# Float64 weights converted in pieces of twice the size, in place, with new lists of steps (Mamba2 SSD, then a SwiGLU feed-forward)

## The chip, the cores and the metric

The kernel runs on one core of one Trainium2 chip. The metric is the device time of one execution in microseconds. The kernel before was timed four times: 417.78, 417.67, 417.70 and 418.24 us, a median of 417.74.

## The reference, cut to what matters

Inputs: x (4, 8, 768, 32), a (4, 8, 768), B and C (4, 8, 768, 16) in float32; the three weight matrices arrive in float64, that is in words of eight bytes, and the gain rms_g in float32. The first part is a state-space recurrence, worked in chunks of 32 here (any size of chunk gives the same values):

```python
for c in range(nc):
    cum = np.cumsum(la, axis=-1)                          # la = log a in the chunk
    L = np.exp(cum[..., :, None] - cum[..., None, :]) * causal
    M = np.einsum('bhin,bhjn->bhij', Cc, Bc) * L
    y[:, :, sl] = (np.einsum('bhij,bhjd->bhid', M, xc)
                   + np.einsum('bhin,bhnd->bhid', Cc, state) * np.exp(cum)[..., None])
    Bx = np.einsum('bhjn,bhjd->bhjnd', Bc, xc) * np.exp(cum[..., -1:] - cum)[..., None, None]
    state = np.exp(np.sum(la, -1))[:, :, None, None] * state + np.sum(Bx, axis=2)
```

The second part takes y as 3072 tokens of 256 numbers:

```python
xn = x / np.sqrt(np.mean(x * x, -1, keepdims=True) + 1e-6) * rms_g
g = xn @ w_gate                                           # 256 x 1536
out = (g / (1 + np.exp(-g)) * (xn @ w_val)) @ w_out       # 1536 x 256
```

## The kernel before, in words

**Tiles and blocks.** The recurrence is worked in 12 pairs of 128-token chunks, the feed-forward in six blocks of 512 tokens, so two pairs make a block. While a block's feed-forward runs, the recurrence of the next block's two pairs is put between its matmuls; block 0 does the first four pairs itself. All code is one function with many small nested ones, and nothing is ordered by a scheduler: every block has a hand-written **list of steps** (block 0 at L950, block 1 at L1022, blocks 2 to 4 at L1049, block 5 at L1075). A step is a word such as `gate.2`; the loop at L978 (L1096 for the other blocks) calls its function, which issues the step's instructions to the queues of their engines. Each engine runs its own queue in the order of the list and waits where an operand, or the space for a result, isn't ready.

**The steps of the recurrence** (pair p, half or chunk i): `d`/`c` sums of logarithms (L329, L339), `dx`/`cx` their exponentials on ACT (L332, L343); `mask`, `sums`, `exp` the decay matrix of half a pair (L363; L374 and L379; ACT L386); `turn` transposes B and C through PE (L434), `T`, `Tt` copy the result out (L440, L442; DVE L912 in pair 0, ACT L909 after it); `g` and `gg` the products C times B (L468), `L` and `L1` their product with the decays (DVE L478, L489); `A` and `S` the states (PE L501; DVE L513, L519 to L523); `y` the outputs (L541, L550); `sq`, `yt` take y out. `scale` multiplies B and C by decays (DVE L419). For later pairs the decays come from memory instead: `row` and `rowout` write sums to DRAM, `spread` (a DMA on SP's queue, L393) reads them back, `sub` and `ex` make the decays of them.

**Norm and feed-forward of block 0.** `ms`, `mc`, `mt`, `rs`, `rb`, `rc`, `xn` make the normalised tokens (PE L591, ACT L597, PE L600, DVE L605 and POOL L607, PE L613, ACT L618, DVE L629). `early` (PE L658) multiplies the first two column blocks of the weights with tokens not yet normalised, and `norm` (DVE L669) puts the factor on afterwards. `gate.f` (PE L648, eight passes of 128x512) makes gate and value of 128 columns, `silu.f` (ACT L674 or L676) and `hid.f` (DVE L681) the hidden rows. For the second half of the columns (j = 3 to 5), as in all later blocks, the product is made of seven half-size products with sums before and after: `cw` (DVE L702) makes sums of weights, `tx` (DVE L709) differences of tokens; `P.k.j` (PE L732) one product, `take` (ACT L738) and `C` (DVE L744) its totals, `silug` (ACT L753) and `hidg` (DVE L757) the hidden rows. `o` (PE L764) is the last projection of block 0; the later blocks project with `O` (PE L815), from sums of weights `two` (DVE L778) and of hidden rows `s` to `s4` (DVE L788 to L798).

**Weights.** A piece of the float64 matrices is fetched as 32-bit words (`fetch`, L134, SP's queue) and converted in three steps: `pow.k` makes the power of two out of the top 16 bits (three ACT instructions, L167, L168, L170); `man.k` makes the mantissa (DVE L177 puts the top 20 bits in place, DVE L180 adds the low word); `wt.k` multiplies the two into the weight tile (DVE L186) and issues the next fetch. There are 20 pieces: four of 128x256 numbers and sixteen of 128x512, each of one matrix only. Nine are fetched at the start. The mantissa has a tile of its own (`m`, two slots); the fetched words have slots of their own (`ws`, four; `wr`, six), the powers four (`e`).

**Slots that make waits.** PSUM is split into three slots of two banks, used in turn by `mask`, `g`, `y`, `early`, `gate` (`take` at L870 picks the slot that was left first, `leave` gives it back), and two single banks ("one", L82) used in turn by `turn`, `A`, `ms`, `rb`, `row`, the sums of logarithms and two of the four results of `gg`. Two of the three slots are handed over to the `P` products by `switch`. A step that takes a slot waits until the reader of the earlier tenant is done: `gate` for an `exp` or a `silu`, a `turn` for the DVE step that read the bank. `load.p` issues six DMAs with the inputs of pair p (L107, L113).

**Start.** `make_identity`, masks and constants are made on DVE and POOL (L210 to L260), each in a tile of its own; 12 matmuls of zeros (L266) run before the first inputs have landed.

Of the kernel before, what the change touches and what calls it, by code (L numbers as in the profile page):

```python
# [9 lines left out]
FP32 = mybir.dt.float32  # L10
I32 = mybir.dt.int32
I16 = mybir.dt.int16
U32 = mybir.dt.uint32
BF16 = mybir.dt.bfloat16
# [6 lines left out]
def kernel(  # L21
# [98 lines left out]
    def words(w):  # L120
# [7 lines left out]
    wdst = {"g": wg, "v": wv, "o": wo}  # L128
    pieces = [(n, c, w) for c, w in [(0, 128), (128, 128)] + [(c, 256) for c in range(256, DF, 256)]
              for n in "gv"]  # L130
    pieces += [("o", c, 2) for c in range(0, NF, 2)]
    fetched = []

    def fetch(k=1):  # L134
        for _ in range(min(k, len(pieces))):
            n, c, w = pieces.pop(0)
            if n == "o":
                src, dst, shape = wsrc[n][:, c:c + w], wo[:, c:c + w], (w, DM)
            else:
                src, dst = wsrc[n][:, :, 2 * c:2 * (c + w)], wdst[n][:, :, c:c + w]  # L140
                shape = (2, w)
            small = shape[0] * shape[1] == 256
            r = raw.tile([P, shape[0], 2 * shape[1]], I32, tag="ws" if small else "wr",
                         name="wr", bufs=4 if small else 6)
            nc.sync.dma_start(out=r, in_=src)
            w32 = r.rearrange("p k (f w) -> p k f w", w=2)
            w16 = r.bitcast(I16).rearrange("p k (f w) -> p k f w", w=4)
            fetched.append((w16[:, :, :, 3], (w32[:, :, :, 0], w32[:, :, :, 1]), dst,
                            [P] + list(shape)))
# [10 lines left out]
    def power(k):  # L160
        words16, (lo, hi), dst, shape = fetched[k]
        n = shape[1] * shape[2]
        e = cvt.tile([P, n], FP32, tag="e", name="e", bufs=4)
        k16 = e.bitcast(I16)[:, n:2 * n].rearrange("p (a b) -> p a b", a=shape[1])
        g = e.rearrange("p (a b) -> p a b", a=shape[1])
        b16 = e.bitcast(I16)[:, 0:n].rearrange("p (a b) -> p a b", a=shape[1])
        nc.scalar.activation(out=k16, in_=words16, func=AF.Relu, scale=1.0 / 16, bias=kinks[:, 0:1])  # L167
        nc.scalar.activation(out=g, in_=k16, func=AF.Prelu, scale=-1.0, bias=kinks[:, 1:2],  # L168
                             alpha=2.0 ** -20)
        nc.scalar.activation(out=b16, in_=g, func=AF.Prelu, scale=-2.0 ** 27, bias=kinks[:, 2:3],  # L170
                             alpha=2.0 ** -20)
        parts[k, "e"] = b16.bitcast(BF16)

    def mantissa(k):
        words16, (lo, hi), dst, shape = fetched[k]
        m = cvt.tile(shape, I32, tag="m", name="m")
        nc.vector.tensor_scalar(out=m, in0=hi, scalar1=0xFFFFF, scalar2=0x100000,  # L177
                                op0=ALU.bitwise_and, op1=ALU.bitwise_or)
        parts[k, "f"] = f = m.bitcast(FP32)
        nc.vector.scalar_tensor_tensor(out=f, in0=lo.bitcast(U32), scalar=2.0 ** -32, in1=m,  # L180
                                       op0=ALU.mult, op1=ALU.add)

    def weight(k):
        words16, (lo, hi), dst, shape = fetched[k]
        e, f = parts.pop((k, "e")), parts.pop((k, "f"))
        nc.vector.scalar_tensor_tensor(out=dst, in0=f, scalar=2.0 ** -20, in1=e,  # L186
                                       op0=ALU.mult, op1=ALU.mult)
        fetch()

    warm = const.tile([P, 256], BF16, name="warm")  # L190
# [8 lines left out]
    fetch(2)  # L199
    gcol = const.tile([P, 2], FP32, name="gcol")  # L200
    nc.sync.dma_start(out=gcol, in_=moe_rms_g.rearrange("(t p) -> p t", p=P))
    fetch(4)
    load(2)
    load_x(2)
    fetch(3)
# [6 lines left out]
    ones = const.tile([P, P], FP32, name="ones")  # L212
    nc.vector.memset(ones, 1.0)
    zeros = const.tile([P, P], FP32, name="zeros")
    nc.vector.memset(zeros, 0.0)
    upto = const.tile([P, P], FP32, name="upto")
    nc.gpsimd.affine_select(out=upto, in_=ones, pattern=[[1, P]], compare_op=ALU.is_ge,
                            fill=0.0, base=0, channel_multiplier=-1)
    never = const.tile([P, P], FP32, name="never")
    nc.gpsimd.affine_select(out=never, in_=zeros, pattern=[[1, P]], compare_op=ALU.is_ge,  # L220
                            fill=-2.0 ** 100, base=0, channel_multiplier=-1)
    after = const.tile([P, P], FP32, name="after")
# [72 lines left out]
    mids = const.tile([P, 2, P], FP32, name="mids")  # L295
# [395 lines left out]

    def combine_w(j):
# [436 lines left out]
```

## Time and profile before

The profile was taken in an execution of its own. Its time was 418.28 us; the profiled span, from the first to the last instruction, is 416.6 us of it.

| view | what it shows |
| --- | --- |
| timed runs | 417.67 to 418.24 us, median 417.74 |
| profiled execution | 418.28 us, span 416.6 us, granted clock of PE 0.999 |
| waits that end PE's idle time | one in the chain of the end: PE idle L266 |
| DMA traffic | 27.99 MB, 24.22 read and 3.28 written in HBM |
| conversion on ACT (L167, L168, L170) | 14.3, 13.6 and 13.6 us in 20 instructions each |
| conversion on DVE (L177, L180) | 7.9 and 12.8 us in 20 instructions each |

PE is TensorE, PEld its weight loads, DVE VectorE, ACT ScalarE, POOL GpSimd, SP the engine whose queue issues most DMAs. In the table of windows each row is a stretch of the span, with the busy time of each engine and its instructions in brackets, then PE's granted clock, the busy share of the DMA engines and GB/s. In a group row the columns are line, engine, operation, result and operands, shapes and count, then busy us and mean ns of one, then the engine's idle time before them and what ended it. A timeline row has start, duration, engine, line and operation. The ends of matmuls are modelled, so the distance from one start to the next says more of PE than the busy time does.

### The profile page before, as it was taken

What the parts mean: (1) busy time and instruction counts of PE and PEld (TensorE: products, weight loads), DVE (VectorE), ACT (ScalarE), POOL (GpSimd) and SP (SyncE); (2) the same over time, 40 slices, a digit from 0 to 9 for tenths busy, and PEclk for the clock granted to TensorE, in tenths of its full rate; (3) what the DMA queues carried; (4) which work ended last, traced back from release to release, by engine and by line L of the source; (5) the groups of instructions that cost most, each with busy time, mean ns of one, the idle gap of its engine ahead of it and who ended that gap; (6) DMA issues with size and microseconds to landing.
All of it is one profiled execution on the core that took longest, in us unless ns stands there. A gap on an engine that the chain in (4) does not pass through costs nothing.

```text
span 416.6 us, 7930 instructions
## 1 busy us (share of the span) xinstructions
PE 411.9 (99%) x3100; PEld 345.0 (83%) x3100; DVE 304.1 (73%) x665; ACT 229.7 (55%) x462; POOL 39.0 (9%) x48
## 2 busy tenths in 40 slices
PE   8999999999999999999999999999999999999996
PEld 5665468888878899888899887899888889988896
DVE  5899998979679986376986477795476684547671
ACT  2998998877646316745428645526646521245410
POOL 3020000023000005000013100014100000000000
PEclk9999999999999999999999999999999999999999
DMA  9899849001007122703070502070100000100001
GB/s 110 225 207 174 238 117 364 8 0 51 2 2 151 30 74 40 112 2 101 9 146 25 77 2 101 2 148 6 53 2 0 2 2 1 52 0 2 0 2 50
DMA packets 86564, 27.99 MB, mean 67 GB/s; under 512 B 76000, under 2 KB 80352, under 8 KB 86528
## 3 DMA queue, kind: packets, MB, share of 16 engines
q1 hardware_dynamic: 82368, 27.24, 27.9%
q10 hardware_dynamic: 4160, 0.26, 0.8%
q8 instruction: 24, 0.39, 0.4%
q14 instruction: 12, 0.10, 0.1%
HBM read 24.22 MB, written 3.28 MB: 66 GB/s over the span
## 4 chain that ended last, share of the span: by engine, by line
PE 99%; DVE 0%; issue 0%
PE gate L732 28%; PE o L815 23%; PE val L732 21%; PE o L764 5%; PE g L468 4%; PE gate L648 3%; PE y L550 3%; PE tp L434 2%; PE y L541 2%; PE gate L658 2%; PE e L363 1%; PE A_ps L501 1%; PE e L374 1%; PE rb L613 1%; PE idle L266 1%; PE ms L591 1%
## 5 line engine op out<-in xcount | busy, mean ns | idle before, releaser
L744 DVE TENSOR_TENSOR c<-val,p 128x512 f32<-128x512 f32 x99 | 67.3, 686 | 49.8 <-PE val L732 37.5
L738 ACT COPY p<-gate 128x512 f32<-128x512 f32 x99 | 57.8, 588 | 68.1 <-PE gate L732 62.9
L732 PE MATMUL gate<-tx,sw 128*128 128x256 f32 x264 | 65.0, 382 | 0.0
L732 PEld LDWEIGHTS gate<-tx,sw 128*128 128x128 f32 x264 | 48.7, 190 | 8.2 <-issue 2.0
L757 DVE TENSOR_TENSOR h<-c 128x256 f32<-128x256 f32 x99 | 41.0, 431 | 19.1 <-ACT c L753 19.0
L753 ACT ACTIVATE c<-c 128x256 f32<-128x256 f32 x99 | 38.2, 413 | 11.5 <-DVE c L744 10.7
L732 PE MATMUL val<-xn,sw 128*128 128x256 f32 x132 | 34.1, 383 | 0.0
L732 PE MATMUL val<-tx,sw 128*128 128x256 f32 x132 | 33.9, 384 | 0.0
L815 PE MATMUL o<-wo,h 128*128 128x128 f32 x240 | 33.7, 277 | 0.0
L732 PE MATMUL gate<-tx,wgv 128*128 128x256 f32 x132 | 33.1, 381 | 0.0
L732 PE MATMUL val<-xn,wgv 128*128 128x256 f32 x132 | 33.1, 379 | 0.0
L732 PE MATMUL gate<-xn,wgv 128*128 128x256 f32 x132 | 33.0, 380 | 0.0
L815 PE MATMUL o<-two,s 128*128 128x128 f32 x240 | 32.0, 275 | 0.0
L569 POOL TENSOR_TENSOR sq<-sq 128x256 f32<-128x256 f32 x12 | 10.1, 840 | 226.9 <-ACT sq L568 196.9
L815 PE MATMUL o<-two,h 128*128 128x128 f32 x240 | 30.9, 275 | 0.0
L815 PEld LDWEIGHTS o<-wo,h 128*128 128x128 f32 x240 | 29.9, 192 | 1.0 <-issue 0.6
L815 PEld LDWEIGHTS o<-two,s 128*128 128x128 f32 x240 | 29.9, 192 | 0.3
L827 ACT COPY v<-o 128x256 f32<-128x256 f32 x15 | 5.6, 373 | 43.6 <-PE o L815 43.6
L815 PEld LDWEIGHTS o<-two,h 128*128 128x128 f32 x240 | 28.9, 192 | 0.1
L732 PEld LDWEIGHTS val<-tx,sw 128*128 128x128 f32 x132 | 24.5, 190 | 4.6 <-DVE h L757 1.0
L732 PEld LDWEIGHTS val<-xn,sw 128*128 128x128 f32 x132 | 24.4, 190 | 4.2 <-issue 0.7
L732 PEld LDWEIGHTS gate<-tx,wgv 128*128 128x128 f32 x132 | 24.8, 190 | 3.5 <-issue 0.2
(158 smaller groups left out, 700.7 us busy)
## 6 DMA issues: line engine op xcount, KB each, us to landing
L<-rowd SPq DMA_DIRECT2D x16, 512.0 KB, 4.7
xr<-in_x_dram SPq DMA_DIRECT2D x24, 128.0 KB, 3.5
wr<-in_moe_w_out_dram SPq DMA_DIRECT2D x6, 512.0 KB, 6.7
wr<-in_moe_w_gate_dram SPq DMA_DIRECT2D x5, 512.0 KB, 6.1
wr<-in_moe_w_val_dram SPq DMA_DIRECT2D x5, 512.0 KB, 5.9
out_dram<-ob SPq DMA_DIRECT2D x10, 256.0 KB, 2.1
br<-in_B_dram SPq DMA_DIRECT2D x22, 64.0 KB, 4.2
cr<-in_C_dram SPq DMA_DIRECT2D x22, 64.0 KB, 3.3
```

What stands on the lines that cost most here:

```text
L434: nc.tensor.transpose(out=tp[:, k], in_=src[:, i].rearrange("p h n -> p (h n)"), identity=ident)
L468: nc.tensor.matmul(out=g[:, 256 * i:256 * i + 256], lhsT=T[r, i, 0], rhs=T[r, i, 1:3].rearrange("p t m -> p (t m)"), start=(i == 0), stop= ...
L550: nc.tensor.matmul(out=y[o:o + 32, h // 4, i * P:(i + 1) * P], lhsT=s["x"][:, i, h], rhs=Ls[p][:, i, h], start=opens, stop=True, tile_posi ...
L569: nc.gpsimd.tensor_tensor(out=sqs[blk][:, tk], in0=sq2[:, 0], in1=sq2[:, 1], op=ALU.add)
L648: nc.tensor.matmul(out=gv[:, k], lhsT=w[:, t, fs], rhs=xns[0][:, t], start=(t == 0), stop=(t == 1))
L732: nc.tensor.matmul(out=dst[:, half[w]], lhsT=lhsT, rhs=rhs, start=(k in (1, 2, 5) and w == 0), stop=True, skip_group_check=True)
L738: nc.scalar.copy(out=t, in_=Xs[j])
L744: nc.vector.tensor_tensor(out=t, in0=Zs[j], in1=a, op=ALU.add)
L753: nc.scalar.activation(out=u, in_=src[:, half[0]], func=AF.Silu)
L757: nc.vector.tensor_tensor(out=hidden_tile(blk, j)[:, c // 10 - 1, c % 10 - 1], in0=u, in1=src[:, half[1]], op=ALU.mult)
L764: nc.tensor.matmul(out=o, lhsT=hs_[blk, f // 2][:, f % 2, k // 2, (k % 2) * P:(k % 2 + 1) * P], rhs=wo[:, f], start=opens, stop=(f == NF - ...
L815: nc.tensor.matmul(out=o[:, t * P:(t + 1) * P], lhsT=lhsT[:, t], rhs=rhs, start=(k in (1, 2, 4, 5) and j == 0 and t == 0), stop=True, skip ...
```

## The change

**Pieces.** Ten pieces in the place of twenty: two of 128x512 numbers and eight of 128x1024. Gate and value of the same columns make one piece, filled by two DMAs; the output matrix comes in pieces of four rows of blocks, not two. Five pieces are fetched at the start, and a new one only after `wt.2` and later ones. Small pieces lie in the slots of the hidden rows ("h"), large ones in three slots ("wr"), the powers in two; the tiles that `take` fills have four slots of their own ("p"). The numbers behind `pow`, `man` and `wt` now count these pieces.

**Mantissas.** They get no tile: both DVE instructions write into the fetched words, every second word of the tile, the first over the high and the second over the low words.

**Constants and sums.** Seven early constants (the zeros of the first matmuls, `ones`, `zeros`, `upto`, `never`, `after`, `mids`) become parts of one tile in the slot of the output tile "ob". The six tiles with sums of weights (`cw.0` to `cw.2` and three `two`) lie in pairs in three slots of "wr".

**Lists.** All four lists of steps are new. Apart from `pow`, `man` and `wt` with numbers from 10 on, block 0 has the same steps as before, and the others have them too. In the diff below the list of block 0 is shown up to the steps of pair 3's outputs; the other lists, the rest of the constants and the new form of two operand choices (L809 to L813) are left out.

```diff
-    wdst = {"g": wg, "v": wv, "o": wo}
-    pieces = [(n, c, w) for c, w in [(0, 128), (128, 128)] + [(c, 256) for c in range(256, DF, 256)]
-              for n in "gv"]
-    pieces += [("o", c, 2) for c in range(0, NF, 2)]
+    pieces = [("gv", c, 128) for c in (0, 128)] + [("gv", c, 256) for c in range(256, DF, 256)]
+    pieces += [("o", c, 4) for c in range(0, NF, 4)]
     fetched = []
 
     def fetch(k=1):
         for _ in range(min(k, len(pieces))):
             n, c, w = pieces.pop(0)
+            if w == 128:
+                r = ffn.tile([P, 8 * w], I32, tag="h", name="wr", bufs=NF // 2)
+            else:
+                r = raw.tile([P, 8 * 256], I32, tag="wr", name="wr", bufs=3)
             if n == "o":
-                src, dst, shape = wsrc[n][:, c:c + w], wo[:, c:c + w], (w, DM)
+                nc.sync.dma_start(out=r.rearrange("p (o m) -> p o m", o=w),
+                                  in_=wsrc[n][:, c:c + w])
+                dst = wo[:, c:c + w].rearrange("p o m -> p (o m)")
             else:
-                src, dst = wsrc[n][:, :, 2 * c:2 * (c + w)], wdst[n][:, :, c:c + w]
-                shape = (2, w)
-            small = shape[0] * shape[1] == 256
-            r = raw.tile([P, shape[0], 2 * shape[1]], I32, tag="ws" if small else "wr",
-                         name="wr", bufs=4 if small else 6)
-            nc.sync.dma_start(out=r, in_=src)
-            w32 = r.rearrange("p k (f w) -> p k f w", w=2)
-            w16 = r.bitcast(I16).rearrange("p k (f w) -> p k f w", w=4)
-            fetched.append((w16[:, :, :, 3], (w32[:, :, :, 0], w32[:, :, :, 1]), dst,
-                            [P] + list(shape)))
+                both = r.rearrange("p (n t f) -> p n t f", n=2, t=2)
+                for k, name in enumerate("gv"):
+                    nc.sync.dma_start(out=both[:, k], in_=wsrc[name][:, :, 2 * c:2 * (c + w)])
+                dst = wgv[:, :, :, c:c + w]
+            w32 = r.rearrange("p (f w) -> p f w", w=2)
+            fetched.append((r.bitcast(I16).rearrange("p (f w) -> p f w", w=4)[:, :, 3],
+                            w32[:, :, 0], w32[:, :, 1], dst, w32.shape[1]))
...
-        words16, (lo, hi), dst, shape = fetched[k]
-        n = shape[1] * shape[2]
-        e = cvt.tile([P, n], FP32, tag="e", name="e", bufs=4)
-        k16 = e.bitcast(I16)[:, n:2 * n].rearrange("p (a b) -> p a b", a=shape[1])
-        g = e.rearrange("p (a b) -> p a b", a=shape[1])
-        b16 = e.bitcast(I16)[:, 0:n].rearrange("p (a b) -> p a b", a=shape[1])
+        words16, lo, hi, dst, n = fetched[k]
+        e = cvt.tile([P, n], FP32, tag="e", name="e", bufs=2)
+        k16, b16 = e.bitcast(I16)[:, n:2 * n], e.bitcast(I16)[:, 0:n]
         nc.scalar.activation(out=k16, in_=words16, func=AF.Relu, scale=1.0 / 16, bias=kinks[:, 0:1])
-        nc.scalar.activation(out=g, in_=k16, func=AF.Prelu, scale=-1.0, bias=kinks[:, 1:2],
+        nc.scalar.activation(out=e, in_=k16, func=AF.Prelu, scale=-1.0, bias=kinks[:, 1:2],
                              alpha=2.0 ** -20)
-        nc.scalar.activation(out=b16, in_=g, func=AF.Prelu, scale=-2.0 ** 27, bias=kinks[:, 2:3],
+        nc.scalar.activation(out=b16, in_=e, func=AF.Prelu, scale=-2.0 ** 27, bias=kinks[:, 2:3],
                              alpha=2.0 ** -20)
-        parts[k, "e"] = b16.bitcast(BF16)
+        parts[k] = b16.bitcast(BF16)
+
 
     def mantissa(k):
-        words16, (lo, hi), dst, shape = fetched[k]
-        m = cvt.tile(shape, I32, tag="m", name="m")
-        nc.vector.tensor_scalar(out=m, in0=hi, scalar1=0xFFFFF, scalar2=0x100000,
+        words16, lo, hi, dst, n = fetched[k]
+        nc.vector.tensor_scalar(out=hi, in0=hi, scalar1=0xFFFFF, scalar2=0x100000,
                                 op0=ALU.bitwise_and, op1=ALU.bitwise_or)
-        parts[k, "f"] = f = m.bitcast(FP32)
-        nc.vector.scalar_tensor_tensor(out=f, in0=lo.bitcast(U32), scalar=2.0 ** -32, in1=m,
-                                       op0=ALU.mult, op1=ALU.add)
+        nc.vector.scalar_tensor_tensor(out=lo.bitcast(FP32), in0=lo.bitcast(U32),
+                                       scalar=2.0 ** -32, in1=hi, op0=ALU.mult, op1=ALU.add)
 
     def weight(k):
-        words16, (lo, hi), dst, shape = fetched[k]
-        e, f = parts.pop((k, "e")), parts.pop((k, "f"))
+        words16, lo, hi, dst, n = fetched[k]
+        f, e = lo.bitcast(FP32), parts.pop(k)
+        if len(dst.shape) > 2:
+            f, e = [v.rearrange("p (n t f) -> p n t f", n=2, t=2) for v in (f, e)]
         nc.vector.scalar_tensor_tensor(out=dst, in0=f, scalar=2.0 ** -20, in1=e,
                                        op0=ALU.mult, op1=ALU.mult)
-        fetch()
-
-    warm = const.tile([P, 256], BF16, name="warm")
+        if k > 1:
+            fetch()
+
+
+    start = ffn.tile([P, 8, P], FP32, tag="ob", name="start", bufs=1)
+    warm = start[:, 0].bitcast(BF16)
...
         load_x(p)
-    fetch(2)
+    fetch(1)
     gcol = const.tile([P, 2], FP32, name="gcol")
     nc.sync.dma_start(out=gcol, in_=moe_rms_g.rearrange("(t p) -> p t", p=P))
-    fetch(4)
+    fetch(2)
     load(2)
     load_x(2)
-    fetch(3)
+    fetch(2)
     load(3)
     load_x(3)
 
 
     ident = const.tile([P, P], FP32, name="ident")
...
+    spaces = []
+
+    def piece_for_sums(k):
+        while len(spaces) <= k // 2:
+            spaces.append(raw.tile([P, 2, 8 * P], FP32, tag="wr", name="sums", bufs=3))
+        return spaces[k // 2][:, k % 2]
+
     def combine_w(j):
         if j < NF // 4:
-            s = raw.tile([P, 2, 4, P], FP32, tag="wr", name="sw", bufs=6)
+            s = piece_for_sums(j).rearrange("p (w k m) -> p w k m", w=2, k=4)
...
-        vs[k, j] = t = cvt.tile([P, 512], FP32, tag="e", name="p", bufs=4)
+        vs[k, j] = t = cvt.tile([P, 512], FP32, tag="p", name="p", bufs=4)
...
-        two[j0 // 2] = w = raw.tile([P, 4, 2, P], FP32, tag="wr", name="two", bufs=6)
+        two[j0 // 2] = w = piece_for_sums(3 + j0 // 2).rearrange("p (k j m) -> p k j m", k=4, j=2)
...
     order = """
-        load.4 mask.0.0 r.0 parts.0 c mask.0.1 turn.0.1 cx T.0.1 Tt.0.1.0 turn.0.0 sums.0.1 cc d
-        turn.1.1 exp.0.1 Tt.0.1.1 sums.0.0 T.0.0 Tt.0.0.0 Tt.0.0.1 dx T.1.1 mask.1.1 scale.1
-        Tt.1.1.0 Tt.1.1.1 exp.0.0 turn.1.0 g.0.1 last.1 T.1.0 sums.1.1 Tt.1.0.0 scale.0 g.0.0
-        last.0 L.0.1 Tl.1 Tt.1.0.1 A.0 exp.1.1 L.0.0 Tl.0 man.0 mask.1.0 pow.0 g.1.1 S.0 row.1
-        pow.1 L.1.1 sums.1.0 A.1 wt.0 exp.1.0 g.1.0 S.1 pow.2 y.0 sq.0 pow.3 r.1 L.1.0 man.1 y.1
-        yt.0 wt.1 sq.1 ydone.0 early.0.0 man.2 rowout.1 pow.4 parts.1 scale.2 ms.0 yt.1 mask.2.0
-        mc.0 turn.2.0 T.2.0 man.3 Tt.2.0.0 pow.5 sums.2.0 ydone.1 mt.0 exp.2.0 early.0.1
-        mask.2.1 sums.2.1 rs.0 wt.2 wt.3 rb early.1.0 exp.2.1 man.4 rc Tt.2.0.1 man.5 mask.3.1
-        sums.3.1 exp.3.1 wt.4 man.6 early.1.1 xn.0 wt.5 load.5 pow.6 mask.3.0 turn.2.1 row.0
-        sums.3.0 norm.0 T.2.1 tx.0 exp.3.0 Tt.2.1.0 Tt.2.1.1 silu.0 scale.3 norm.1 rowout.0
-        gate.2 pow.7 wt.6 man.7 gg.2 silu.2 hid.0 man.8 L.2.0 hid.2 gate.3 L1.2.2 spread.8 wt.7
-        turn.3.0 gate.4 pow.8 silu.3 L1.2.3 wt.8 pow.9 man.9 T.3.0 spread.9 hid.3 Tt.3.0.0
-        silu.1 A.2 Tt.3.0.1 wt.9 switch.0 man.10 gate.5 turn.3.1 pow.10 man.11 silu.4 cw.3 wt.10
-        pow.11 hid.4 P.1.3 S.2 silu.5 T.3.1 take.1.3 spread.10 y.2 Tt.3.1.0 wt.11 A.3 hid.5
-        Tt.3.1.1 man.12 P.1.4 man.13 pow.12 gg.3 S.3 P.6.3 yt.2 sq.2 ydone.2 switch.1 P.2.3
-        spread.11 pow.13 take.1.4 L1.3.2 L.3.0 take.6.3 L1.3.3 P.2.4 y.3 tok P.7.3 C.11.3 cw.4
...
+        mask.0.1 r.0 d parts.0 c turn.0.0 T.0.0 Tt.0.0.0 turn.0.1 sums.0.1 turn.1.0 T.0.1
+        mask.0.0 Tt.0.0.1 Tt.0.1.0 dx sums.0.0 cx Tt.0.1.1 g.0.0 exp.0.1 T.1.0 turn.1.1 Tt.1.0.0
+        scale.1 mask.1.1 exp.0.0 T.1.1 Tt.1.1.0 cc scale.0 L.0.0 Tt.1.0.1 sums.1.1 g.0.1
+        Tt.1.1.1 A.0 g.1.1 exp.1.1 mask.1.0 pow.0 L.0.1 S.0 last.0 g.1.0 last.1 L.1.1 Tl.0
+        sums.1.0 Tl.1 A.1 exp.1.0 y.0 man.0 r.1 sq.0 S.1 pow.1 L.1.0 wt.0 y.1 yt.0 ydone.0
+        parts.1 scale.2 sq.1 early.0.0 pow.2 yt.1 man.1 mask.2.0 ms.0 mc.0 wt.1 sums.2.0 row.1
+        ydone.1 early.0.1 mt.0 mask.2.1 rs.0 sums.2.1 turn.2.0 rowout.1 exp.2.0 mask.3.1 man.2
+        exp.2.1 rb early.1.0 rc T.2.0 xn.0 Tt.2.0.0 norm.0 sums.3.1 early.1.1 wt.2 Tt.2.0.1
+        pow.3 mask.3.0 exp.3.1 man.3 turn.2.1 row.0 T.2.1 Tt.2.1.0 sums.3.0 rowout.0 scale.3
+        exp.3.0 Tt.2.1.1 pow.4 wt.3 gate.2 norm.1 gg.2 silu.0 pow.5 gate.3 load.4 A.2 man.4
+        L.2.0 silu.3 L1.2.2 hid.0 wt.4 spread.8 S.2 silu.2 gate.4 hid.3 L1.2.3 switch.0 silu.1
+        turn.3.1 hid.2 turn.3.0 T.3.0 silu.4 P.1.3 T.3.1 Tt.3.0.0 man.5 Tt.3.1.0 hid.4 take.1.3
+        Tt.3.0.1 gate.5 table Tt.3.1.1 tx.0 silu.5 cw.3 wt.5 hid.5 cw.4 pow.6 y.2 P.1.4 A.3
+        P.6.3 yt.2 take.6.3 gg.3 sq.2 S.3 man.6 P.7.3 take.1.4 L1.3.2 take.7.3 L.3.0 pow.7
+        ydone.2 switch.1 L1.3.3 P.2.3 P.6.4 C.11.3 y.3 P.5.3 take.6.4 wt.6 P.4.3 tok man.7
+        silug.21.3 P.2.4 yt.3 silug.11.3 hidg.21.3 P.7.4 sq.3 P.1.5 ms.1 C.22.3 hidg.11.3
+        take.1.5 P.3.3 C.11.4 cw.5 wt.7 tokout take.7.4 C.12.3 P.5.4 silug.11.4 spread.9 ydone.3
+        P.6.5 P.2.5 C.22.4 silug.22.3 silug.12.3 hidg.11.4 take.6.5 C.11.5 P.3.4 hid.1 mc.1
...
```

## The prediction, on record before the changed kernel had run

> **What bounds the kernel now.** I read the busy table first. TensorE (PE) is busy for the whole span; VectorE (DVE) for 73%, ScalarE (ACT) for 55%.
>
> ```profile
> span 416.6 us, 7930 instructions
> PE 411.9 (99%) x3100; PEld 345.0 (83%) x3100; DVE 304.1 (73%) x665; ACT 229.7 (55%) x462; POOL 39.0 (9%) x48
> ```
>
> A busy PE row may hide pauses, since matmul ends are modelled, so I took start-to-start times from the timeline instead. A 128x256 matmul pass follows the last after 0.216 us (L732, 924 passes, mean 0.221), a 128x128 one after 0.112 us (L815), a 128x512 one after 0.43 us (L648). Added up by these, the second to last stretches are almost pure matmul work: block 5 (358 to 413 us) loses 0.1 us, blocks 1 to 4 lose 2.8 to 3.6 us each, nearly all at changes of tile shape (0.25 us after the eight L541 passes, 0.2 us around the L468 group). Block 0 (0 to 99.2 us) holds 84.4 us of matmul work and loses 13.7, about 9 of it in the first 30 us. So PE is the bound nearly everywhere, and only block 0 can give or take anything. (The Trainium skill, "Perfetto Trace Analysis", section Identifying the Most-Contended Engine, calls matmul busy time a bad measure of headroom and prefers LDWEIGHTS busy, here 83%. By that rule 17% would be open; the spacing shows it is not, as a 0.19 us load hides behind each 0.216 us pass.)
>
> Next the ten-microsecond windows of block 0: which engine has no room beside PE?
>
> ```profile
> 20.00:30.00 10.00, 10.00 (x131) 6.46 (x124) 9.72 (x26) 9.28 (x17) 2.62 (x3) 1.00 0.89 208
> 30.00:40.00 10.00, 10.00 (x57) 6.21 (x57) 9.86 (x20) 8.47 (x14) 0.00 (x0) 1.00 0.90 130
> 40.00:50.00 10.00, 10.00 (x47) 4.65 (x47) 9.88 (x17) 9.74 (x18) 0.00 (x0) 1.00 1.03 308
> 50.00:60.00 10.00, 10.00 (x104) 6.22 (x103) 9.27 (x20) 9.80 (x18) 0.73 (x1) 1.00 0.29 46
> ```
>
> Third and fourth busy numbers are DVE and ACT: both are full from 20 to 60 us. PE keeps going there only because the list of steps hands it work just in time. One place shows it failing, the L468 group at 57 us, which takes 1.75 us instead of 1.08 because its bank waits for L513:
>
> ```profile
> 57.00 1.82 PE L468 MATMUL g<-T 32*128 32x256 f32 x16
> 57.35 0.28 DVE L513 TENSOR_TENSOR A<-A_ps,tmask 128x128 f32<-128x128 f32 x1
> 57.69 0.72 PEld L468 LDWEIGHTS g<-T 32*128 32x128 f32 x10 [0.39 <-DVE A L513]
> ```
>
> **The change, part by part.** *Pieces.* The conversion costs, by shape:
>
> ```profile
> L167 ACT ACTIVATE e<-wr,kinks 128x512 int16<-128x512 int16 x16 | 12.3, 766 | 0.0
> L180 DVE SCALAR_TENSOR_TENSOR m<-wr,m 128x512 f32<-128x512 uint32 x16 | 11.1, 693 | 0.5
> L177 DVE TENSOR_SCALAR m<-wr 128x512 int32<-128x512 int32 x16 | 6.7, 422 | 0.1
> L167 ACT ACTIVATE e<-wr,kinks 128x256 int16<-128x256 int16 x4 | 2.1, 520 | 0.0
> L180 DVE SCALAR_TENSOR_TENSOR m<-wr,m 128x256 f32<-128x256 uint32 x4 | 1.7, 425 | 0.1
> ```
>
> Start to start, a 256 piece takes 0.99 us of DVE and 1.52 of ACT, a 512 piece 1.66 and 2.17. Carrying the slopes on, 1024 takes 3.0 (0.72 + 1.145 + 1.135) and 3.5. Before: 4 x 0.99 + 16 x 1.66 = 30.5 us of DVE, 4 x 1.52 + 16 x 2.17 = 40.8 of ACT. After, 2 pieces of 512 and 8 of 1024: 27.3 and 32.3. So 3.2 us of DVE and 8.5 us of ACT go. None of it is on PE, so the gain by itself is nothing; what counts is when each engine reaches the step that PE waits for. The price of size: one weight step now holds ACT for 3.5 us without a break.
>
> *Mantissas in place.* Both results now go to every second word of the fetched tile. Reads with that stride are in the rows above (422 ns); writes are not. Bounds: no loss, or the tensor_scalar falls from its double slope (0.14 us per 256, against 0.27 of L180) to the single one, 1.2 us as the 128x1024 tensor_tensor (1214 ns), +0.5 us a piece; as far as the row goes the loss cannot exceed a doubling of both, +1.9 us a piece. A gain I exclude: the element count is the same. I take no loss, being nearest to the strided read. (The Trainium skill, "VectorE: DVE Perf Modes", What auto-detection actually checks, asks for one source and a destination in SBUF with even outer sizes for the double rate and names no stride; by it the step is 0.7 us, and no run here has shown the write.)
>
> *Fetching.* A slot is free only after the last weight step, with three large slots. Piece 5 is issued at about 35.5 us, after wt.2, and ACT wants it at 44: 8.5 us against landings of 3.8 to 9.5 us (median 5.7). Hidden at the median; at the worst landing 1 us late. The six issues of load.4 move behind piece 6 and are wanted some 30 us later. spread.8 waits on SP's queue for y.2 (56 us), with pieces 8 and 9 behind it; these are wanted after 75 us. Constants in the output slot add no instruction: the slot is next written at 99 us.
>
> *Lists.* The listing of both kernels shows the same matmuls by kind and count. Counting the shape changes by the losses above, blocks 1 to 5 come to 12.30 us before and 12.26 after: nothing. Their waits stay as covered as before, since ACT and DVE have 2 to 5 us idle per ten there. Block 0 I worked along its order, each step with its row's spacing and 0.1 to 0.25 us for a hand-over (row.0 ends at 8.73, PE starts on it at 8.98).
>
> 1. Start. PE now does d before c and the turns, so turn.0.0 stands behind dx on ACT: d (1.28 us at this slow start) ends at 7.8, dx 8.5, turn.0.0 9.2, turn.0.1 after cx 9.7, turn.1.0 behind Tt.0.0.1 10.95. g.0.0 ends at 13.0, with 5.78 us of list work done; before, 6.48 were done by 13.24. **Late by 0.45 us**, still 0.44 at y.1's end (23.55 against 23.32, 16.77 us of work against 16.98).
> 2. Gate.2. mc.0 now stands behind pow.2 (24.5 to 28.0), mt.0 follows early.0.1 at 28.6, so rs on POOL (1.26 us) and rb come at 30.85, rc ends 31.95. pow.3 follows (32.7 to 36.2) and exp.3.1 behind it ends at 37.15; gate.2 needs that slot. PE is there at 36.8 and starts at 37.35. Before it started at 36.64.
> 3. Hid.3. After exp.3.0 ACT runs pow.4, the table load (1.28), silu.0, pow.5, 38.85 to 47.65, and only then silu.3 (48.15). DVE has finished S.2 by 46.8 and stands idle 1.45 us for it. turn.3.1 needs L1.2.3 behind hid.3: PE is there at 49.1 and starts at 49.7.
> 4. Y.3. From 48.25 DVE is full: hid.3, L1.2.3, hid.2, man.5, hid.4, tx.0, cw.3, wt.5, hid.5, cw.4, S.3, man.6, L1.3.2, L.3.0, L1.3.3 are 7 x 0.6 + 2 x 1.87 + 3 x 1.47 + 1.14 + 0.85 + 1.13 = 15.5 us, so y.3 starts at 63.85 with 54.0 us of work done, offset 9.85. Before: 61.2, 53.1, offset 8.1. **Late by 1.7 us.** tx.0 and two cw steps (4.4 us) stand ahead of S.3 and L1.3.3 here; before, tx.0 and cw.4 did not stand there.
> 5. Later DVE and ACT reach each matmul's need 3 us or more ahead, thanks to the saved 3.2 and 8.5 us; PE gives nothing back, as it was already full there.
>
> Sum: +1.7. My hand-overs lean to the long side over about four of them, so I take +1.5. The profiled execution's own time is 418.28 (span 416.57 and 1.71 around it); by it the changed kernel would take 419.8. It stands 0.54 above the median 417.74, so against medians I forecast **419.2 us**.
>
> **Rivals.**
> A. *ACT keeps up.* If silu.3 is done by 46.6 instead of 48.15 (shorter long activations, or rc earlier), DVE never idles at step 3 and L1.3.3 comes 1.45 us sooner: +0.1 to +0.3, 417.9. From a lead of 0.9 us on, the result is within the bound. For: before, ACT had spare time at 32 to 33 us. Against: three 3.5 us pieces in 15 us. This is the case on the other side: not slower.
> B. *Strided writes at single rate.* man.5 and man.6 lie in the full chain of step 4: 2 x 0.5 = +1.0, 420.2; with both operations doubled, 2 x 1.9 = +3.8, 423.0. For: no row shows such a write. Against: the strided read costs nothing.
> C. *Everything in time.* Rival A, and the start on time (-0.45) and no wait at L513 (-0.67): 416.8. This needs three separate things.
> D. *A late landing of piece 5* (9.5 us): +1.0, 420.2.
> E. *Twice the size saves nothing* (cost per element only): 8 x 0.3 us more DVE by piece 9, of which two pieces before y.3: +0.6, 419.8. The 256 and 512 rows speak against it.
>
> **Numbers.** The measurement tells about 0.2% (0.84 us) from no change: faster is below 416.9, slower above 418.58. Forecast 0.43 (418.6 to 420.0); A 0.26; B, D and E 0.17; C 0.14. Slower 0.60, same 0.26, faster 0.14. The range leaves out the far half of B and most of C: 417.0 to 421.2.
>
> **What would show it.** 128x1024 rows of 0.7, 1.2 and 1.2 us on DVE, 1.2 us on ACT; DVE idle before the L683 steps near 47 us, ended by ACT; y.3 near 64 us; block lengths after it as before (64.4 us). Wrong: y.3 before 62.5, or a loss inside blocks 1 to 4.

## The result, and the profile after

After: a median of 418.66 us in 32 runs (418.34 to 429.16). Before, beside it: 418.24 in 50 runs (417.50 to 418.63). The ratio is **1.0023, 95% interval 1.0017 to 1.0028**, or +0.96 us (0.7 to 1.2): slower by a quarter of a per cent. The ratio goes by means; the medians stand only 0.42 us apart, because, by their times, 27 of the 50 executions of before had the long start told of below and 19 of after's 31 the short one. The forecast was +1.46. One execution of after (429.16 us) and one of run 4 (429.68) lie over 2% above the others of their kernel and are left out of the ratios.

One thing is needed to read the numbers: PE's first passes run at half their rate until 5.6 us at the latest in six of the 14 profiled executions (one of each kernel), and until 9 to 10 us in the other eight. The profiled execution of before has the long start, that of after the short one. "Like for like" below compares medians of executions with the same start; it puts after 0.86 us (short) and 1.43 us (long) behind before.

The busy table and the chain of the end, after:

```profile
span 416.9 us, 7846 instructions
PE 410.3 (98%) x3100; PEld 343.9 (82%) x3100; DVE 308.9 (74%) x635; ACT 223.4 (54%) x434; POOL 41.4 (10%) x48
PE 91%; ACT 4%; DVE 3%; issue 1%; DVEq 0%; ACTq 0%
```

ACT lost 6 us of work and 28 instructions, DVE lost 30 instructions, and the span did not shrink. The chain of the end was 99% PE before; now 8% of it is ACT, DVE or issue, so PE waits for them somewhere early. The conversion, one instruction per row:

```profile
L165 ACT ACTIVATE e<-wr,kinks 128x1024 int16<-128x1024 int16 x8 | 10.0, 1252 | 0.0
L177 DVE SCALAR_TENSOR_TENSOR wr<-wr 128x1024 f32<-128x1024 uint32 x8 | 9.8, 1229 | 0.3
L185 DVE SCALAR_TENSOR_TENSOR wgv<-wr,e 128x1024 f32<-128x1024 f32 x5 | 6.1, 1215 | 0.0
L175 DVE TENSOR_SCALAR wr<-wr 128x1024 int32<-128x1024 int32 x8 | 5.5, 693 | 0.0
```

The forms are as cheap as the slopes said: 693 ns against 422 for half the size, in place and strided. DVE's busy time rose all the same, by 4.8 us; run 1 below has 305.4, so 3.5 of these come with the list of blocks 2 to 4. The windows of block 0 (after PE and its loads come DVE and ACT):

```profile
20.00:30.00 10.00, 9.92 (x111) 6.72 (x110) 9.71 (x19) 8.41 (x11) 2.51 (x3) 1.00 1.00 255
30.00:40.00 10.00, 9.84 (x59) 5.94 (x62) 9.23 (x14) 9.79 (x15) 0.00 (x0) 1.00 0.73 166
40.00:50.00 10.00, 10.00 (x51) 5.05 (x44) 8.06 (x12) 9.07 (x13) 0.00 (x0) 1.00 0.94 221
50.00:60.00 10.00, 9.32 (x100) 5.43 (x99) 9.79 (x21) 9.10 (x15) 0.55 (x1) 1.00 0.47 172
```

DVE was at 9.88 in 40 to 50 us and is at 8.06: it stands idle there, and then PE falls to 9.32 in the next ten. Three rows of the timeline say why:

```profile
47.01 0.69 DVE L683 TENSOR_TENSOR h<-u,gate 128x512 f32<-128x512 f32 x1 [1.70 <-ACT u L676]
...
54.38 1.22 DVE L185 SCALAR_TENSOR_TENSOR wgv<-wr,e 128x1024 f32<-128x1024 f32 x1
...
55.65 1.13 PE L741 MATMUL gate<-xn,wgv 128*128 128x256 f32 x4 [0.68 <-DVE wgv L185]
```

`hid.3` waits 1.70 us for ACT's silu; later `wt.5`, queued behind that and behind `tx.0` and `cw.3`, ends only at 55.60, and `P.1.4` has stood 0.68 us for it. The wait in the g group that was shown of before is gone: its 16 passes start at 58.13 us and the next product at 59.20, the full-speed 1.07.

The rest is seen in the lengths of the blocks, from the first matmul of one to that of the next. "Lost" is what the distances between starts hold beyond the passes' own spacing; in blocks 1 to 5 it lies at changes of tile shape, but for short waits of 0.25 us in block 1 of before and 0.19 in its block 3.

| block | length before | after | lost before | lost after |
| --- | --- | --- | --- | --- |
| 0 | 98.12 (long start) | 97.90 (short), 98.85 (long, run 1) | 14.50 | 14.28, 15.23 |
| 1 | 65.16 | 64.91 | 3.59 | 3.34 |
| 2 | 64.40 | 64.65 | 2.80 | 3.04 |
| 3 | 64.34 | 64.54 | 2.90 | 3.09 |
| 4 | 64.67 | 64.91 | 3.10 | 3.34 |
| 5 | 54.91 | 54.91 | 0.06 | 0.06 |

Block 0 is +0.73 at the long start, block 1 -0.25, blocks 2 to 4 together +0.69, the end after the last matmul +0.1. That is +1.27, against +1.43 in the times.

### The profile page after: what moved, and what is told of

It reads as the page before. It is cut to its first block, busy times and chain, and to the rows that moved or that the text cites. A ratio compares the mean times of both kernels' runs of the same rounds, so it can differ in the third digit from the quotient of the medians.

```text
span 416.9 us, 7846 instructions
## 1 busy us (share of the span) xinstructions
PE 410.3 (98%) x3100; PEld 343.9 (82%) x3100; DVE 308.9 (74%) x635; ACT 223.4 (54%) x434; POOL 41.4 (10%) x48
## 4 chain that ended last, share of the span: by engine, by line
PE 91%; ACT 4%; DVE 3%; issue 1%; DVEq 0%; ACTq 0%
PE gate L741 28%; PE o L826 23%; PE val L741 21%; PE o L773 5%; PE g L470 3%; PE y L552 2%; PE tp L436 2%; PE y L543 1%; PE gate L660 1%; PE A_ps L503 1%; PE e L365 1%; ACT e L166 1%; ACT e L165 1%; PE idle L268 1%; PE rb L615 1%
## 5 line engine op out<-in xcount | busy, mean ns | idle before, releaser
L741 PE MATMUL gate<-tx,sw 128*128 128x256 f32 x144 | 36.4, 382 | 0.0
L826 PE MATMUL o<-sums,h 128*128 128x128 f32 x240 | 32.7, 276 | 0.0
L826 PE MATMUL o<-sums,s 128*128 128x128 f32 x240 | 31.8, 277 | 0.0
L741 PEld LDWEIGHTS gate<-tx,sw 128*128 128x128 f32 x144 | 27.0, 190 | 4.6 <-issue 0.7
L826 PEld LDWEIGHTS o<-sums,h 128*128 128x128 f32 x240 | 29.6, 192 | 0.6 <-DVE h L766 0.5
L741 PE MATMUL gate<-tx,sums 128*128 128x256 f32 x120 | 30.0, 379 | 0.0
L826 PEld LDWEIGHTS o<-sums,s 128*128 128x128 f32 x240 | 29.1, 192 | 0.8 <-issue 0.8
L741 PEld LDWEIGHTS gate<-xn,wgv 128*128 128x128 f32 x132 | 23.5, 190 | 5.3 <-DVE h L766 1.5
L741 PEld LDWEIGHTS val<-xn,wgv 128*128 128x128 f32 x132 | 25.1, 190 | 3.4
L762 ACT ACTIVATE u<-gate 128x256 f32<-128x256 f32 x33 | 12.3, 382 | 24.2 <-PE gate L741 24.2
```

Source lines behind the costliest of these rows:

```text
L741: nc.tensor.matmul(out=dst[:, half[w]], lhsT=lhsT, rhs=rhs, start=(k in (1, 2, 5) and w == 0), stop=True, skip_group_check=True)
L762: nc.scalar.activation(out=u, in_=src[:, half[0]], func=AF.Silu)
L826: nc.tensor.matmul(out=o[:, t * P:(t + 1) * P], lhsT=lhsT[:, t], rhs=rhs, start=(k in (1, 2, 4, 5) and j == 0 and t == 0), stop=True, skip ...
```

## The experiments

My theory after reading the traces was that the time comes from two places: the list of blocks 2 to 4, and DVE's queue in block 0, which now has `tx.0`, `cw` and `wt.5` ahead of what PE wants. The rivals were the new start, and the larger pieces themselves, so that smaller ones would be better. Ratios are to before, with the 95% interval.

**1 and 2. The list of blocks 2 to 4, each way round.** Run 1 is after with the old list, run 2 is before with the new one. The part of it that carries PE's order, for run 1:

```diff
-  ... scale.1 ... g.0 ... C.22.0 P.4.1 P.3.1 P.1.2 turn.1.1 P.3.0 ... A.0 P.1.3 ...
-  ... L.1 P.7.4 A.1 take.7.5 take.7.4 P.4.5 ... P.3.4 y.1 O.4.0 ...
+  ... g.0 ... P.5.1 scale.1 ... P.3.0 ... P.1.3 ... P.3.1 hid.22.0 A.0 turn.1.1 ...
+  ... P.3.5 ... A.1 silu.11.5 ... S.1 y.1 P.3.4 ...
```

> The changed kernel with the list of blocks 2 to 4 of the kernel before. Theory A: a good part of the loss lies in those three blocks, where matmul starts in the profile of the changed kernel show 64.65, 64.53 and 64.91 us against 64.40, 64.34 and 64.67 before, at changes of tile shape and without a wait. Then this kernel is 0.6 to 0.75 us faster than the changed one, about 0.3 us slower than the kernel before. Theory B, as the prediction counted: blocks 1 to 5 are equal in both, and block 0 holds the whole loss. Then this kernel takes the changed kernel's time within 0.1 us.

> The kernel before with the changed list of blocks 2 to 4 and nothing else. Theory A: 0.6 to 0.75 us slower than the kernel before. Theory B: no change within 0.1 us.

Measured: run 1 418.51, ratio 1.0014 (1.0004 to 1.0023), 0.62 us below after like for like; blocks 2 to 4 take 64.48, 64.34 and 64.67. Run 2 418.79, ratio 1.0019 (1.0010 to 1.0027), blocks 2 to 4 at 64.65, 64.54 and 64.91, the last matmul 0.66 us later than in before. The list alone carries these 0.7 us, with small pieces or large ones. (Run 2 is 1.0 us slower like for like, 0.3 more than PE's matmuls show. That part lies outside the span: run 2's times are 2.0 us above their spans, those of before 1.7. Why stays open.) The whole stretch of block 2, before and after:

```profile
164.39:228.79 64.40, 64.40 (x515) 56.39 (x514) 45.87 (x99) 33.81 (x70) 6.54 (x7) 1.00 0.34 66
```

```profile
163.92:228.57 64.65, 64.65 (x516) 56.36 (x515) 48.16 (x97) 34.01 (x72) 9.16 (x9) 1.00 0.27 58
```

PE is busy in all of both, so nothing here is a wait that a busy column could show. It can be read from starts alone. Around `A.1` and `y.1`, PE's rows of before, then of after:

```profile
204.02 1.03 PE L732 MATMUL val<-xn,sw 128*128 128x256 f32 x4
204.98 0.43 PE L501 MATMUL A_ps<-xr,Bd 128*32 128x64 f32 x16
205.34 0.45 PE L541 MATMUL y<-T,S 32*64 32x128 f32 x8
```

```profile
205.88 1.03 PE L741 MATMUL val<-xn,sw 128*128 128x256 f32 x4
206.84 0.45 PE L543 MATMUL y<-T,S 32*64 32x128 f32 x8
```

Four passes of 0.216 are 0.86 us; the next shape starts after 0.96. In before y follows A directly; in after A stands alone between products, and y pays an entry of its own. So does A, and both pay on the way out, as the first product behind A shows, where four passes again take 0.96 (after):

```profile
201.97 0.43 PE L503 MATMUL A_ps<-xr,Bd 128*32 128x64 f32 x16
202.33 1.13 PE L741 MATMUL gate<-tx,wgv 128*128 128x256 f32 x4
203.29 1.03 PE L741 MATMUL val<-tx,sw 128*128 128x256 f32 x4
```

Read pass by pass, blocks 1 to 5 of both kernels keep the same prices. The last pass with the full array (128*128 in the rows) ahead of a part of it (32*128, 128*32, 32*64) takes 0.09 us more than its spacing; the first product or projection behind a part takes 0.10 more, a transpose behind a part 0.05. From one full shape to another nothing is added, and between two steps that both use a part neither price is paid. Both lists change shape equally often (29 times in block 2), but each of blocks 2 to 4 goes between full array and part 12 times in the old list and 14 times in the new one: 0.20 us, and 0.05 more because a product and not a transpose now follows the first A. That is 0.25 of the measured 0.25 in block 2 and 0.24 in block 4; in block 3, where before waits 0.19 us in its ms step and saves a change between A and y, 0.20 is measured.

**3. The lists of after with pieces of the old size.** Each `pow`, `man` and `wt` works two halves, one after the other.

```diff
-    pieces = [("gv", c, 128) for c in (0, 128)] + [("gv", c, 256) for c in range(256, DF, 256)]
-    pieces += [("o", c, 4) for c in range(0, NF, 4)]
+    pieces = [(n, c, w) for c, w in [(0, 128), (128, 128)] + [(c, 256) for c in range(256, DF, 256)]
+              for n in "gv"]
+    pieces += [("o", c, 2) for c in range(0, NF, 2)]
...
+    def both(step):
+        return lambda k: (step(2 * k), step(2 * k + 1))
...
-        "pow": power, "man": mantissa, "wt": weight,
+        "pow": both(power), "man": both(mantissa), "wt": both(weight),
```

> The changed kernel with its lists, but each piece fetched and converted as two halves, one after the other within the same step (128x256 and 128x512 as before the change). DVE gets 0.33 us more for each large piece and ACT 0.85 us. Theory A (DVE and ACT set the order of block 0 between 43 and 62 us): three to four pieces lie ahead of the outputs of pair 3, so this is 1.0 to 1.5 us slower than the changed kernel. Theory C: the size of the pieces is worth nothing, as neither engine ends last: within 0.2 us of the changed kernel.

Measured: 424.07, ratio 1.0139 (1.0125 to 1.0153), 4.4 us above after like for like, three times what was expected; all of it in block 0, at 103.48 us. The size is worth a lot under these lists; blocks 1 to 5 keep after's lengths to 0.01. Against run 1, which has the same start, PE is 1.8 us late at `gate.2`, 3.5 at `turn.3.1` and 4.5 at `y.3`. The wait for `silu.3` grows, in the same place:

```profile
51.45 0.69 DVE L682 TENSOR_TENSOR h<-u,gate 128x512 f32<-128x512 f32 x1 [2.45 <-ACT u L675]
```

**4, 5 and 6. The DVE queue before y.3**: `wt.5` ahead of `tx.0` and `cw.3` (4), `man.6` behind `L1.3.3` (5), both (6).

```diff
-  ... Tt.3.1.1 tx.0 silu.5 cw.3 wt.5 hid.5 ...
+  ... Tt.3.1.1 wt.5 tx.0 silu.5 cw.3 hid.5 ...
-  ... S.3 man.6 P.7.3 ... switch.1 L1.3.3 P.2.3 ...
+  ... S.3 P.7.3 ... switch.1 L1.3.3 man.6 P.2.3 ...
```

> The changed kernel with step wt.5 put ahead of tx.0 and cw.3 in the list of block 0. The profile of the changed kernel shows PE waiting 0.7 us for L185 (wt.5) at P.1.4. Theory D (a wait with a place of its own): the wait goes and the time falls by 0.5 to 0.7 us. Theory E (the DVE work ahead of the outputs of pair 3 is the same in any order, and pair 3's outputs start when it is done): P.1.3 and y.2 keep their times, y.3 starts where it did, and the time stays within 0.2 us.

> The changed kernel with step man.6 moved from behind S.3 to behind L1.3.3 in the list of block 0; nothing else. In the profile of the changed kernel man.6 holds DVE from 58.3 to 60.2 us, while the products L1.3.2, L.3.0 and L1.3.3 that y.3 waits for stand behind it; PE loses 0.9 us at y.3, of which 0.4 us is change of tile shape (0.38 at the same place before). Theory F: PE then finds y.3 ready, and the time falls by 0.4 to 0.5 us. Theory G: the work is only displaced, piece 6 is late for P.1.5 and PE loses the same there: within 0.2 us of the changed kernel.

> Both moves in the changed kernel: wt.5 ahead of tx.0 and cw.3, man.6 behind L1.3.3. Moving wt.5 alone freed 0.75 us at P.1.4 and lost 1.25 us of it again before y.3, 0.5 of them because L177 of man.6 took 1.73 us in the place of 1.23 while a POOL operation ran. Theory F (a full DVE ahead of y.3): with man.6 out of the way both gains stay, 1.1 to 1.3 us less than the changed kernel. Theory G (displaced only): within 0.3 us of the changed kernel.

Measured: 420.25 (1.0042, 1.0028 to 1.0057), 420.59 (1.0052, 1.0040 to 1.0065) and 419.26 (1.0034, 1.0021 to 1.0048); like for like 0.55, 0.8 and 0.15 us above after. Each frees its wait and loses it again. With `wt.5` early `P.1.4` starts 0.75 us sooner, but `gg.3` then waits for `S.3` behind `cw.4`, and `y.3` comes 0.5 us later, because `man.6` takes longer:

```profile
58.95 0.73 POOL L571 TENSOR_TENSOR sq<-sq 128x256 f32<-128x256 f32 x1 [29.95 <-issue]
59.03 1.73 DVE L177 SCALAR_TENSOR_TENSOR wr<-wr 128x1024 f32<-128x1024 uint32 x1
```

That is run 4; in after DVE came first, and POOL paid:

```profile
59.04 1.23 DVE L177 SCALAR_TENSOR_TENSOR wr<-wr 128x1024 f32<-128x1024 uint32 x1
59.45 1.40 POOL L571 TENSOR_TENSOR sq<-sq 128x256 f32<-128x256 f32 x1 [30.46 <-issue]
```

With `man.6` late, `C.11.3` stands behind it and `P.5.3` waits 0.86 us (run 5):

```profile
65.49 1.13 PE L741 MATMUL val<-tx,sw 128*128 128x256 f32 x4 [0.86 <-DVE c L753]
```

**7. The new pieces under all of the old lists**: after's conversion and slots, before's order; its converted weights are other ones, since `man.k` stands ahead of `pow.k` there for most pieces and now overwrites the exponent bits that `pow` reads.

```diff
-  (the four lists of after)
+  (the four lists of before, with the new numbers of pow, man and wt)
```

> The changed kernel's pieces, mantissas, slots and constants with all four lists of the kernel before; in block 0 two steps of a kind (pow, man, wt) that converted two halves become one: pow and man where the first half stood, wt where the second stood (the first for the output matrix). Theory I (the lists hold the loss, the size is a gain that needs a list): DVE is relieved by 0.33 us and ACT by 0.85 us a piece, and the 0.67 us that PE waited for L513 at the second products of pair 3 go: 0.2 to 0.7 us faster than the kernel before. Theory H (the size holds a loss): three ACT instructions of 3.5 us without a break stand ahead of the silu steps, and block 0 is 1 us or more longer than before.

Measured: 439.18, ratio 1.0502 (1.0489 to 1.0516). What was expected missed it by far. The waits of SP's queue from 40 to 80 us (line, what it waited for: us in total, times, longest) and the timeline:

```profile
SPq L113 <- PE y L543: 16.3, 1, 16.3
SPq L395 <- DMA rowd<-r_sb: 1.7, 1, 1.7
```

```profile
65.32 0.39 SPq L146 DMA_DIRECT2D wr<-in_moe_w_gate_dram  x1
...
72.03 0.70 DVE L175 TENSOR_SCALAR wr<-wr 128x1024 int32<-128x1024 int32 x1 [12.85 <-DMA wr<-in_moe_w_val_dram]
```

With three slots a fetch can no longer run ahead of the list. One input DMA of `load.5` waits 16.3 us on the queue for pair 2's y, a `spread` behind it 1.7 us for the sums it reads, and the fetch behind both is issued only at 65.32; DVE stands 12.85 us for its words. Another `spread` then holds the queue for 10.5 us from 67.5 on, and the next fetch is issued at 82.15. So the new list of block 0 was not a tuning beside the change but a condition of it: `load.4` and `load.5` had to go behind the fetches, and `pow` ahead of `man`. (How much of the 21 us each of these waits makes was not measured.)

**8. The old order of the start**, up to `y.1`, with after's other steps. `man.0` stands ahead of `pow.0` here, so the first piece's weights are other ones.

```diff
-  mask.0.1 r.0 d parts.0 c turn.0.0 T.0.0 Tt.0.0.0 turn.0.1 sums.0.1 turn.1.0 ...
+  mask.0.0 r.0 parts.0 c mask.0.1 turn.0.1 cx T.0.1 Tt.0.1.0 turn.0.0 sums.0.1 cc d ...
```

> The changed kernel with the steps up to y.1 in the order of the kernel before (the first two PSUM slots change names, so that the later steps find theirs). Starts of matmuls show passes at half rate up to 5.7 us in some executions and up to 9.3 us in others; from the same state of that, early.0.0 stands 0.4 us earlier in the changed kernel than before where it warms early, and equal where it warms late. Theory J (the new start is a small gain, the loss lies behind it): this kernel is 0 to 0.4 us slower than the changed one, and its executions differ by 0.55 us between the two, not by 0.95. Theory K, the prediction's step 1 (the new start costs 0.45 us): 0.45 us faster than the changed kernel.

Measured: 419.19, ratio 1.0035 (1.0023 to 1.0047); like for like 0.55 slower than after with the short start, equal with the long one. The new start costs nothing; it gains half a microsecond whenever PE reaches its full rate early.

**9 to 12. A better version?** Run 9 makes four moves in block 0, run 10 adds the old lists of blocks 2 to 5, run 11 moves `man.7` and `wt.7` too, run 12 puts `man.5` into DVE's idle time ahead of `hid.3` and `man.7`, `wt.7` a little later than run 11 does.

```diff
+  9:  Tt.3.1.1 wt.5 tx.0   S.3 cw.4   C.11.3 man.6   hidg.12.5 cw.0
+  10: 9, and the lists of blocks 2 to 5 of before
+  11: 10, and C.22.4 man.7 wt.7
+  12: 10, and S.2 man.5   C.11.5 hid.1 man.7 wt.7
```

> The changed kernel with four steps of block 0 moved: wt.5 ahead of tx.0, cw.4 from ahead of S.3 to behind it, man.6 from behind S.3 to behind C.11.3, cw.0 from ahead of hidg.21.5 to behind hidg.12.5. Runs so far: man.6 directly behind L1.3.3 made P.5.3 wait 0.86 us for C.11.3, and gg.3 waited for S.3 behind cw.4. Theory F (DVE is the second bound of block 0, and PE waits where a step that nobody needs yet stands ahead of one that PE needs): P.1.4 0.75 us earlier, gg.3 the same, y.3 about 1.0 and P.5.3 about 1.2 us earlier, and 1.0 to 1.3 us less at the end. Theory G (DVE's whole work to the end of block 0 sets the end, in any order): later steps lose it again, within 0.3 us of the changed kernel.

> The same four moves, and the lists of blocks 2 to 5 of the kernel before. Theories A and F together: 0.67 us less in blocks 2 to 4, about 0.1 at the end, 1.0 to 1.3 in block 0, so 1.8 to 2.1 us less than the changed kernel and 0.8 to 1.1 us less than the kernel before. Theory G: 0.7 us less than the changed kernel, 0.2 us more than the kernel before.

> The kernel of the four moves with the lists of blocks 2 to 5 from before, and two moves more: man.7 and wt.7 from ahead of hidg.21.3 and C.12.3 to behind C.22.4. In the profile without them PE was 1.32 us earlier at P.7.4 than in the changed kernel and lost it at P.1.5 (0.6 us, waiting for hidg.21.3 behind man.7), P.2.5 (0.6, waiting for C.12.3 behind wt.7) and P.3.4 (0.1). Theory F (order on a full DVE): the 1.3 us stay, the time is 1.1 to 1.4 us less than with four moves, 0.7 to 0.9 us less than the kernel before. Theory G (DVE's whole work): o.0, C.11.5 or the last hidg steps then wait, and the time stays within 0.3 us of the kernel with four moves.

> The kernel of the four moves with the lists of blocks 2 to 5 from before, and: man.5 from behind turn.3 into the 1.7 us that DVE spends idle ahead of hid.3 (it waits for silu.3 behind pow.5), and man.7 and wt.7 behind C.11.5 and hid.1. With six moves, man.7 and wt.7 ahead of C.11.5 made PE wait 0.96 us at P.5.5. Theory F with a full DVE: only DVE time that stood idle can move the end. 1.7 us of it are filled here, so wt.5 and all DVE steps behind it come up to 1.5 us earlier, the wait at P.5.5 goes, and turn.3.1 is late by at most 0.3: 0.6 to 1.1 us less than with six moves, 0.4 to 1.0 us less than the kernel before. Theory G (something else than DVE ends block 0): within 0.2 us of the kernel with six moves.

Measured: 419.91 (1.0038, 1.0024 to 1.0052), 418.25 (1.0007, 0.9998 to 1.0016), 417.93 (1.0009, 0.9999 to 1.0019) and 419.21 (1.0027, 1.0017 to 1.0036). Like for like against after: +0.26, -0.4, -0.7 and -0.4, of which the lists of blocks 2 to 4 are -0.62 in the last three. In run 10 PE is 1.32 us ahead at `P.7.4` and gives all of it back at the next two things it takes from DVE:

```profile
66.95 1.13 PE L741 MATMUL gate<-xn,wgv 128*128 128x256 f32 x4 [0.41 <-DVE h L766]
...
71.68 1.13 PE L741 MATMUL val<-xn,wgv 128*128 128x256 f32 x4 [0.46 <-DVE c L753]
```

In run 12 it is 1.08 us ahead up to `P.5.5`, and then `o.0` waits for `wt.7`:

```profile
74.90 1.23 DVE L185 SCALAR_TENSOR_TENSOR wo<-wr,e 128x1024 f32<-128x1024 f32 x1
76.18 1.99 PE L773 MATMUL o<-wo,h 128*128 128x256 f32 x8 [0.97 <-DVE wo L185]
```

None is faster than before. Run 11 comes nearest, not told from before by its interval, but like for like 0.1 (short) to 0.8 us (long) above it. Without the lists of blocks 2 to 4 these moves change after by +0.3 to -0.1 us: no run got the 0.73 us of block 0 back, so that they lie in the order of DVE's queue is read from the waits and not shown by a run. DVE still stands idle for 1.3 us between 69 and 72 us in run 12; whether an order that puts `man.7` exactly there would pay was not tried.

## Why the prediction came out as it did

Sign, range and rough size were right, but two errors partly cancelled, and that the number came so near is luck: at the long start, from which the prediction was worked, block 0 gives +0.73 where +1.5 was forecast, and the rest +0.54 where nothing was. One of its own signs of being wrong came, a loss inside blocks 1 to 4. The 0.54 us by which the profiled execution stood above the median were the long start.

- **Step 1, "late by 0.45 us": wrong.** The start of `early.0.0` less the PE work before it is 9.88 us in both kernels at the long start. At the short one it is about 0.95 us less in after, and 0.4 less in run 8. Run 8 tells it apart: with the old start back, the kernel is no faster. I had put the slow passes of one execution into the order of all.
- **Step 2, gate.2 behind exp.3.1: right.** PE loses 0.46 us ahead of `gate.2`, against 0.23 before.
- **Step 3, DVE idle for silu.3: right.** 1.70 us for 1.45 predicted, in the place named. `turn.3.1`, which was to wait 0.6 us for it, waits 0.10.
- **Step 4, y.3 at 63.85 and 1.7 us late: mechanism right, size off.** y.3 is at 63.09 at the long start, 0.68 us late, and 0.96 just after it. The first loss is at `P.1.4` for `wt.5`, one step of the same DVE queue, which I had not looked at. My hand-overs were too long and the 0.45 of step 1 was in the sum; and 0.3 of the 1.7 came from reading y.3 of before at 61.2, the start of the product ahead of it, where its row says:

```profile
61.54 1.08 PE L550 MATMUL y<-L,xr 128*32 128x128 f32 x32
```

- **Step 5, nothing given back: nearly.** 0.96 becomes 0.73 by the end of block 0.
- **"Blocks 1 to 5 come to 12.30 us before and 12.26 after: nothing": this step failed.** They lose 12.45 and 12.87, +0.42. I gave each kind of shape change one price; what costs time is going from the full array to a part of it and back, and the new list of blocks 2 to 4 does so 14 times a block, not 12. Runs 1 and 2 show that this list alone makes +0.7. Block 1 makes -0.25 in every run with its new list.
- **Rivals.** B (strided writes at the single rate) is dead: 693 ns. D did not occur: no ACT or DVE step of piece 5 waits for its landing. E is dead too: 693 and 1229 ns are less than twice 422 and 693. A fails because ACT did not keep up at silu.3; of C's three things two came, the start on time and no wait at the g group.

**Where the expected gain went.** ACT's total was never a bound, only its order at `silu.3`. DVE, with 3 us less conversion, gets to block 1's preparation sooner. The windows 99 to 105 us, before, then after:

```profile
99.00:105.00 6.00, 6.00 (x31) 5.06 (x30) 5.91 (x12) 4.18 (x9) 1.90 (x2) 1.00 0.27 90
```

```profile
99.00:105.00 6.00, 6.00 (x31) 5.26 (x30) 3.32 (x9) 4.24 (x8) 0.00 (x0) 1.00 0.58 118
```

DVE falls from 5.91 to 3.32 of 6 us, and PE is full in both rows: the saved time lands where PE did not wait for it. Much of the fall is work done earlier: up to 99 us DVE is busy for 89.45 us after and 87.57 before, up to 105 us for 92.77 and 93.48.

Block 1's -0.25 is not at shape changes: it goes between full array and part 14 times in both lists. Two short waits of PE for ACT are gone, 0.10 us for a `take` and 0.13 for a copy that ends inside a g group, which takes 1.28 us here and 1.15 elsewhere (before):

```profile
102.68 0.73 PEld L732 LDWEIGHTS gate<-tx,sw 128*128 128x128 f32 x4 [0.23 <-ACT p L738]
...
134.48 0.37 ACT L909 ACTIVATE T<-tp,tmask 128x128 f32<-128x128 f32 x1
134.75 1.28 PE L468 MATMUL g<-T 32*128 32x256 f32 x16
```

It comes with the new list, for the most part at least: with small pieces (run 3) block 1 takes 64.91 us too, and with large ones under the old list (run 7) 65.06.

## What to carry to other kernels

A saving on engines beside a full PE is worth only the waits it removes; follow the order of the queue of the fullest other engine, and for each matmul ask which step behind which other step it takes its operand from: freeing one such step hands the wait to the next. When lists of a PE-bound stretch are reordered, count how often the list goes from the full array to a part of it and back, not how often the shape changes, and measure the list alone in the old kernel. Writing over an operand in place also orders all its readers, and fewer slots for a transfer bind its issue to everything queued ahead of it.

## What the runs showed that was not expected

**The start of PE.** Run 1 has the same steps at the start as after; its profiled execution has the long slow phase, that of after the short one. The first two passes, after, then run 1:

```profile
5.51 0.67 PE L306 MATMUL r_ps<-start,la 128*128 128x256 f32 x2
```

```profile
5.51 1.19 PE L306 MATMUL r_ps<-start,la 128*128 128x256 f32 x2
```

Same code, same start, 0.67 or 1.19 us. The row of granted clocks reads full speed from the first slice on in both, so only durations tell it. The timed runs of every kernel but run 7's (four, with no clear groups) fall into two groups, and each profiled execution's start agrees with the group its time falls into. The medians of the groups are 417.76 and 418.29 for before, 418.62 and 419.72 for after, 419.17 and 419.68 with the old start (run 8). The gap is 0.5 us with the old start and 1.1 with the new. That it is because `d`, `c` and the first transposes now stand in the slow phase with the chain behind them is read from the rows, not tested. The Trainium skill, "TensorE: Matmul & The Clock Gate", Part 1, What's actually happening, says PE begins at half its rate until a free-running window of about 3.4 us has been busy, and gives plus or minus 500 ns for the moment. The half rate agrees; the moments here, 5.6 us at the latest and 9 to 10 us, are about a whole window apart.

**DVE beside POOL.** The two pairs of rows under runs 4 to 6 show it: whichever of the two starts first keeps its time (1.23 for `man.6`, 0.73 for `sq`), and the other takes longer (1.73, 1.40). The Trainium skill, "SBUF — State Buffer", Who interferes with whom, says a DVE instruction with two operands in SBUF contends with a POOL instruction that reads there, and that the order of issue decides which of the two is held up. Both pairs agree. A move of 0.1 us in a DVE queue can thus change the length of what it moves.
